# Token groups 4 to 7 normalized in the written order with GpSimd's help, and the token-block steps hung on named units

## The chip, the cores and the metric

The kernel runs on one core of a Trainium2 chip. A core has five engines that work side by side, each through its own queue in order: TensorE (PE in the profile, its weight loads PEld), VectorE (DVE), ScalarE (ACT), GpSimd (POOL) and SyncE (SP), which here only issues DMAs; POOL issues DMAs too. The metric is the device time of one execution in microseconds (us), the median of three executions.

## What is computed

The input `x` has 2048 tokens of 640 channels. It is normalized per token (mean and variance over the 640 channels, no learned scale), and the result `xn` feeds two branches whose sum is added to `x`:

```python
xn = _layernorm(x, axis=-1)
a = einsum("bsd,ed->bse", xn, dft_hid_re);  b = einsum("bsd,ed->bse", xn, dft_hid_im)
y = einsum("ts,bse->bte", dft_seq_re, a) - einsum("ts,bse->bte", dft_seq_im, b)
gate = xn @ W_gate;  up = xn @ W_up                      # 640 -> 1728
out = x + y + ((gate * (gate > 0)) * up) @ W_down        # 1728 -> 640
```

All data are float32. The kernel multiplies in a split form: an operand is divided into a high part (an ACT copy rounded to `float32r`) and a low part (the rest, by a DVE subtraction, `split`, lines 123 to 125), and a product is three matmuls, high by high, high by low, low by high (`mm3`, lines 130 to 132).

## The kernel before, in words

**Three stages.** The first (to about 405 us) multiplies the two 2048x2048 sequence matrices with `xn`; the second is gate and up; the third is the projection by `W_down` and by the hidden matrices. The change is in the first stage alone.

**Tokens.** A group is 256 tokens (two blocks `j` of 128), so there are 8 groups (`NG`), and `NH` = 4 is half of them. `xn` of groups 0 to 3 lies in `xs_early`, of groups 4 to 7 in `xs_late`, high beside low. The output columns are worked through in 4 chunks `c` of 512.

**Units.** The first stage is a list `todo` of units, each with four steps: `load` (DMAs of 512 KB of a sequence matrix into a tile `raw`, or `tk` for a kept one), `prepare` (the high and low part, into one of the 3 buffers `cb` of the pool `ring`, made by `parts`), `run` (the matmuls) and `finish`. `drive(4, 2)` (line 725) goes through the list: at place i it traces `prepare` of unit i-2, `load` of unit i, `finish` of unit i-5 and `run` of unit i-4, so a unit is prepared two units ahead of its matmuls. `defer(k, f)` calls `f` k places later.

The first 16 units are `B11` (groups 0 to 3) and `B21` (groups 4 to 7), for each group once with chunk c=0 and once with c=1 (`first_stream`, line 546). The two units of a group have 18 matmuls each. The tokens of group g+1 are normalized in `prepare` of unit (c=1, group g). After these come the same units for chunks 2 and 3, and then for each chunk c the units `T1`, `T2`, `B22`, `T3`, `T4` (four each, `stream`, line 644; order in lines 771 to 775). `T1` and `B22` units have 18 matmuls, the others 12. `prepare` of a `T` unit has a DVE subtraction (line 672 and following, recorded at line 646) ahead of the split; that of `B22` has the split alone. After the last of four units `combine` (line 614) does 2 to 4 operations of 128x512 on the sums.

**Who sets the order.** The program is traced in the order above; a planner then lays out each engine's queue, moving an instruction forward where it takes its operands to be ready sooner. Two things hold it: `tc.keep_in_program_order` (through `pin`) puts an instruction behind all that was traced on its engine, and `tc.issue_after(ins)` puts a block's instructions on the engine of `ins` behind `ins`. Neither waits for data by itself.

**The two ways to normalize.** Groups 1 to 3 use `next_group` (line 266), pinned: statistics on DVE (`ln_stats`, lines 204 and 205), the unit's high part on ACT (274), the unit's low part in two halves on POOL (272, for g > 1), held back by `behind_vector` (264) until DVE has finished the low part before it, the root (211 to 218), the normalized high part in two ACT operations (281), the centred and scaled tokens in two DVE operations (285), the low part (287). Groups 4 to 7 use `layernorm` (line 237), which isn't pinned but for the queueing behind `late["ln"]`: one block is centred and scaled by DVE (247), the other by ACT (248), then one ACT copy (251, recorded at 121) and one DVE subtraction (252) of both. In `next_group` the high and low part have 384 of the 640 channels per block (`K14`); the other 256 are moved by a DMA (`keep_a21`, 235). In groups 4 to 7 all 640 are made. The matmuls of the c=0 unit of groups 1 to 3 are `next_products` (line 488, recorded at 495), pinned, which start with what is ready first; those of groups 4 to 7 went through `product`.

**Token-block steps.** Six background steps (`token_sets(1, step)`, line 338) make transposed, normalized blocks that the second stage needs. Steps 0 and 1 load `mr` (mean and root rows, broadcast) and `a` by 3 POOL DMAs, do an add and a multiply of 128x512 (364, 365) and a split; steps 2 to 5 load by 4 POOL DMAs (378, 379), do two adds and two multiplies of 128x512 (384, 385), four subtractions of 128x256 (`more`, 391) and two splits of 128x1024, and store the halves by POOL DMAs (422). Their work tiles lie in eight slots (`work`), used in turn. Before the change a step is put into the list 2 units after `V3` and then every `SPACE` = 9 entries: the load at its place, the halves 6 and 7 units later, all arithmetic in one piece.

Of the kernel before, what the change touches and what calls it, by code (L numbers as in the profile page):

```python
# [12 lines left out]
P = 128  # L13
# [45 lines left out]
def fnet_reglu_kernel(  # L59
# [177 lines left out]
    def layernorm(g):  # L237
        xs, bs, mv = ln_tiles(g)
        js = slice(0, SG)

        with tc.issue_after(late["ln"]):
            for i in ln_stats(g, xs, bs, mv, js):
                pass
            for i in ln_root(g, mv, js):
                late["ln"] = i.ins
            nc.vector.tensor_tensor(mv[:, 1, 6:7], stat[:, 0, g, 1:2], stat[:, 1, g, 1:2], op=OP.mult)
            nc.vector.tensor_scalar(xs[:, 0], xs[:, 0], mv[:, 0, 0:1], stat[:, 1, g, 0:1], op0=OP.subtract, op1=OP.mult)
            nc.scalar.activation(xs[:, 1], xs[:, 1], AF.Identity, bias=mv[:, 1, 6:7], scale=stat[:, 1, g, 1:2])
            cs = K14 if g < NH else slice(0, D)
            src = xs[:, :, cs]  # L250
            high = copy(xn_block(g, cs, 0), src)
            low = nc.vector.tensor_tensor(xn_block(g, cs, 1), src, xn_block(g, cs, 0).bitcast(F32), op=OP.subtract)
            if g < NH:
                keep_a21(g)
        if g == NG - 1:
            nc.sync.dma_start(rows.rearrange("m (g p j) -> p m g j", p=P, j=SG), stat)

# [8 lines left out]
    def next_group(g, b, raw, before):  # L266

        xs, bs, mv = ln_tiles(g)
        js = slice(0, SG)
        nm, r = (stat[:, i, g, js] for i in range(2))  # L270
# [10 lines left out]
        pin(nc.scalar.activation(xn_block(g, K14, 0)[:, j], xs[:, j, K14], AF.Identity,  # L281
# [5 lines left out]
        late["ln"] = pin([nc.vector.tensor_tensor(xn_block(g, K14, 1), xs[:, :, K14], xn_block(g, K14, 0).bitcast(F32),  # L287
                                                  op=OP.subtract)])[0].ins
        keep_a21(g)
# [48 lines left out]
    def token_sets(q, step, place=None, unit=None):  # L338
# [30 lines left out]
        else:  # L369
# [11 lines left out]
            def make():  # L381
                mr, ab = t["mr"], t["ab"]
                for i in range(2):
                    tc.keep_in_program_order(tt(part(ab, i), part(ab, i), part(mr, 0), op=OP.add))  # L384
                    tt(part(ab, i), part(ab, i), part(mr, 1), op=OP.mult)
# [23 lines left out]
        def begin():  # L409
            load()  # L410
            for i, (make, name, place, view) in enumerate(made):

                def halve(make=make, name=name):
                    for m in make:
                        m()
                    src = t[name]
                    t["h" + name] = h = work()[:, : src.shape[1]]
                    split(h.bitcast(F32R), src.bitcast(F32R), src)

                def keep(name=name, place=place, view=view):  # L420
                    for v, part in enumerate((t["h" + name], t[name])):
                        nc.gpsimd.dma_start(place(v), view(part))
# [65 lines left out]
    def next_products(n, b):  # L488

        keys = [("e1", 0), ("e1", 1), "v1"]  # L490
        for js, vs in (((0,), (0, 2)), ((1,), (0, 2)), ((0, 1), (1,))):
            for j in js:
                for v in vs:
                    for d, key in zip((0, 1, 4), keys):
                        start["pe"] = pin([nc.tensor.matmul(E[0, key], xn_part(n * SG + j, d)[v == 1], b[:, int(v == 2), j],  # L495
                                                            start=False, stop=n == NH - 1 and (j, v) == (1, 1))])[0].ins
# [49 lines left out]
    def first_stream(c, name, g):  # L546
# [24 lines left out]
        def prepare():  # L571
# [4 lines left out]
            if (n > 0 or c > 1) and "b" not in t:  # L576
                t["b"] = b = parts()
                with ExitStack() as order:
                    if c == 1 and n < NH:
                        order.enter_context(tc.issue_after(late["ln"]))  # L580
                    i = split(flat(b, 0), flat(b, 1), t["s"])
                if c == 1 and n < NH - 1:
                    late["ln"] = i.ins
            if norm is not None:
                if norm < NH:
                    t1 = start[0, norm]
                    t1["b"] = parts()
                    next_group(norm, t1["b"], t1["s"], flat(b, 1)[:, W2 - 1 : W2] if norm > 1 else None)
                else:
                    layernorm(norm)  # L590

        def run():
# [3 lines left out]
            if 0 < n < NH and c == 0:  # L596
# [3 lines left out]
            with ExitStack() as order:  # L600
                if 0 < n < NH and c == 1:
# [42 lines left out]
    def stream(c, name, g):  # L644
# [19 lines left out]
        def prepare():  # L664
# [4 lines left out]
            with in_turn():  # L669
# [13 lines left out]
                lows.append(split(flat(b, 0), flat(b, 1), src))  # L683

# [55 lines left out]
    steps = [(q, i) for q in (1,) for i in range(SET_STEPS)]  # L740
    early_sets, first_sets = list(SETS_A), list(SETS_B)
    free = [None]
    SPACE = 9

    def phase(c, names):


        for n in names.split():
# [12 lines left out]
            if n == "V3":  # L761
                free[0] = len(todo) + 2
            if free[0] is not None and len(todo) >= free[0] and steps:
                token_sets(*steps.pop(0))
                free[0] = len(todo) + SPACE

# [7 lines left out]
    assert not steps, len(steps)  # L774
    phase(NCHUNK - 1, "T10 T11 T12 T13 T20 B220 T21 B221 T22 T23 K K K A A B222 B223 T30 A T31 A T32 A T33 T40 T41 T42 T43 K")
    assert not early_sets and not first_sets
    drive(4, 2)
    ph1.close()
# [522 lines left out]
```

## Time and profile before

| | |
|---|---|
| median of 3 runs | 1040.99 us (1040.63 to 1042.91) |
| the profiled execution, its own time | 1040.59 us |
| its span in the trace | 1038.7 us |
| TensorE busy | 1025.0 us, 99% |
| VectorE busy | 801.3 us, 77% |
| ScalarE busy | 432.1 us, 42% |
| GpSimd busy | 106.9 us, 10% |
| granted TensorE clock | 1.00 |

How to read the profile: times in the trace count from the start of the span. A row of the timeline has the start, the duration, the engine, the line of the kernel, the operation, output and inputs by the program's names, the shapes, the count, and in brackets the idle time of that engine ahead of it with what ended it. A row of the windows has the stretch, its length, and for each engine the busy time and the number of instructions, then the granted clock, the DMA share and GB/s. A row of the operations of one tile has the count, then the shortest, median and longest duration in ns, and the first and last start in us. Matmuls are pipelined: their rows overlap, so lost time is read from the distance of their starts.

### The profile page before, as it was taken

The numbers are of one execution on the slowest core, as the hardware profiler recorded it, in microseconds if no ns is written. First come the engines' busy times: TensorE is split into PE (matmuls) and PEld (weight loads), VectorE is DVE, ScalarE is ACT, GpSimd is POOL, SyncE is SP. The second block draws the span as 40 slices with busy tenths as digits, with TensorE's granted clock in tenths as the row PEclk, the third lists the DMA queues.
The fourth block names the chain that finished last, engine by engine and source line by source line (L and its number), as shares of the span: only waits on it lengthen the run. The fifth ranks groups of instructions, "written<-read, shape, count | busy, mean of one in ns | idle before, by whom it ended". The sixth has DMA issues, their size and how long they took to land.

```text
span 1038.7 us, 12463 instructions
## 1 busy us (share of the span) xinstructions
PE 1025.0 (99%) x4528; PEld 844.2 (81%) x4528; DVE 801.3 (77%) x1074; ACT 432.1 (42%) x544; POOL 106.9 (10%) x172
## 2 busy tenths in 40 slices
PE   9899999999999999999999999999999999999998
PEld 7788888888787888888888888888878888888886
DVE  7857887979979767688887988887498667786764
ACT  6654453333343423333334534433365423552521
POOL 3211000102121001321110010010000000000000
PEclk9999999999999999999999999999999999999999
DMA  8987743947977975763363666663698636986554
GB/s 303 320 284 258 255 141 115 333 171 251 364 239 273 391 304 190 250 237 136 149 233 135 225 223 237 229 248 122 207 367 292 197 120 217 379 299 219 159 157 122
DMA packets 101468, 242.73 MB, mean 234 GB/s; under 512 B 11552, under 2 KB 50976, under 8 KB 98848
## 3 DMA queue, kind: packets, MB, share of 16 engines
q1 hardware_dynamic: 83664, 171.68, 48.2%
q0 software_dynamic: 17744, 70.26, 18.4%
q8 instruction: 35, 0.57, 0.2%
q14 instruction: 25, 0.20, 0.1%
HBM read 182.12 MB, written 58.74 MB: 232 GB/s over the span
## 4 chain that ended last, share of the span: by engine, by line
PE 91%; DVE 5%; DMA 1%; ACT 1%; issue 1%; SPq 0%; DVEq 0%; ACTq 0%
PE ps L132 30%; PE ps L131 30%; PE ps L130 30%; DVE cb L125 1%; PE ps L1198 1%; PE ps L495 1%; DMA rw<-hd 1%; DVE raw L646 1%; DMA raw<-in_dft 1%; DVE r L125 0%; DVE tk L646 0%; ACT cb L124 0%; DVE bs L204 0%; DVE r L391 0%; DVE r L384 0%
## 5 line engine op out<-in xcount | busy, mean ns | idle before, releaser
L130 PE MATMUL ps<-cb,wt 128*128 128x512 f32 x390 | 151.9, 390 | 0.4 <-ACT wt L124 0.4
L132 PE MATMUL ps<-cb,wt 128*128 128x512 f32 x390 | 151.9, 390 | 0.4 <-DVE wt L125 0.4
L131 PE MATMUL ps<-cb,wt 128*128 128x512 f32 x390 | 151.8, 389 | 0.0
L125 DVE TENSOR_TENSOR cb<-rw,cb 128x1024 fp32r<-128x1024 f32 x83 | 94.1, 1134 | 69.3 <-ACT cb L124 68.7
L124 ACT ACTIVATE cb<-rw 128x1024 fp32r<-128x1024 f32 x83 | 81.9, 987 | 149.9 <-PE ps L132 124.8
L124 ACT ACTIVATE cb<-raw 128x1024 fp32r<-128x1024 f32 x75 | 79.4, 1060 | 132.1 <-PE ps L132 101.6
L125 DVE TENSOR_TENSOR cb<-raw,cb 128x1024 fp32r<-128x1024 f32 x75 | 91.5, 1223 | 42.0 <-ACT cb L124 41.8
L130 PE MATMUL ps<-cb,xs_late 128*128 128x512 f32 x256 | 99.3, 390 | 4.3 <-ACT xs_late L121 2.8
L131 PE MATMUL ps<-cb,xs_late 128*128 128x512 f32 x256 | 100.1, 391 | 1.4 <-DVE cb L125 1.2
L131 PE MATMUL ps<-xs_early,gw 128*128 128x512 f32 x260 | 101.2, 389 | 0.0
L130 PE MATMUL ps<-xs_early,gw 128*128 128x512 f32 x260 | 101.2, 389 | 0.0
L132 PE MATMUL ps<-xs_early,gw 128*128 128x512 f32 x260 | 101.1, 389 | 0.0
L132 PE MATMUL ps<-cb,xs_late 128*128 128x512 f32 x256 | 99.3, 389 | 0.0
L121 ACT ACTIVATE gw<-z 128x1024 fp32r<-128x1024 f32 (+1 forms) x52 | 57.6, 1110 | 77.7 <-DVE z L808 75.1
L132 PE MATMUL ps<-cb,xs_early 128*128 128x512 f32 x226 | 87.9, 389 | 0.0
L131 PE MATMUL ps<-cb,xs_early 128*128 128x512 f32 x226 | 87.9, 389 | 0.0
L130 PE MATMUL ps<-cb,xs_early 128*128 128x512 f32 x226 | 87.4, 390 | 0.4 <-ACT cb L124 0.4
L130 PEld LDWEIGHTS ps<-cb,wt 128*128 128x128 f32 x390 | 73.2, 188 | 16.1 <-ACT wt L124 0.9
L132 PEld LDWEIGHTS ps<-cb,wt 128*128 128x128 f32 x390 | 73.2, 188 | 15.9 <-DVE wt L125 0.7
L131 PEld LDWEIGHTS ps<-cb,wt 128*128 128x128 f32 x390 | 73.2, 188 | 15.7 <-DVE cb L125 0.3
L121 ACT ACTIVATE u<-ps 128x512 f32<-128x512 f32 x52 | 31.1, 599 | 93.7 <-PE ps L132 93.7
L818 DVE TENSOR_TENSOR gw<-z,gw 128x1024 fp32r<-128x1024 f32 (+1 forms) x52 | 64.7, 1286 | 3.8 <-ACT gw L121 3.8
(198 smaller groups left out, 1947.7 us busy)
## 6 DMA issues: line engine op xcount, KB each, us to landing
raw<-in_dft SPq DMA_DIRECT2D x94, 512.0 KB, 6.2
wt<-wparts SPq DMA_DIRECT2D x66, 256.0 KB, 3.2
z<-in_wgu SPq DMA_DIRECT2D x26, 640.0 KB, 3.9
hd<-ob POOLq DMA_DIRECT2D x26, 512.0 KB, 3.7
rw<-hd SPq DMA_DIRECT2D x24, 512.0 KB, 6.8
wparts<-pw POOLq DMA_DIRECT2D x11, 1024.0 KB, 4.1
tk<-in_dft SPq DMA_DIRECT2D x16, 512.0 KB, 7.0
set<-r POOLq DMA_DIRECT2D x16, 512.0 KB, 4.6
```

The lines of the kernel that those rows point to most:

```text
L121: return nc.scalar.activation(o, i, AF.Copy)
L124: nc.scalar.activation(hi, src, AF.Copy)
L125: return nc.vector.tensor_tensor(lo, src, hi.bitcast(F32), op=OP.subtract)
L130: nc.tensor.matmul(ps, wh, mh, start=first, stop=False, skip_group_check=more)
L131: nc.tensor.matmul(ps, wh, ml, start=False, stop=False, skip_group_check=more)
L132: nc.tensor.matmul(ps, wl, mh, start=False, stop=last, skip_group_check=more)
L495: start["pe"] = pin([nc.tensor.matmul(E[0, key], xn_part(n * SG + j, d)[v == 1], b[:, int(v == 2), j], start=False, stop=n == NH - 1 and ( ...
L646: sub = lambda o, i0, i1: nc.vector.tensor_tensor(o, i0, i1, op=OP.subtract)
L818: tt(self.w[:, 1, cs], self.z[:, cs], self.w[:, 0, cs].bitcast(F32), op=OP.subtract)
L1198: nc.tensor.matmul(B[key], wr[:, v, es], hr[:, cs], start=False, stop=v == 1, skip_group_check=not new)
```

## The change

Groups 4 to 7 go through `next_group` and `next_products` as well, over all 640 channels; `layernorm` is gone. With that, the `ring` buffer of the c=0 unit is made there too, its low part goes to POOL, and the queueing of the c=1 unit holds for all groups. The token-block steps are no units of their own any more: their loads, makes, `more`, halves and stores are hung on `prepare` of named units. Steps 0 and 1: load at `T1` units 2 and 3 of chunk 0, the rest at `B22` units 0 and 1 of chunk 0. Steps 2 and 3 (c=1), 4 and 5 (c=2): loads at `T3` unit 3 and `T4` unit 1 of the chunk before, one add and multiply at each `T1` unit of chunk c, `more` and the halves at its `B22` units, stores 2 units later.

```diff
@@ first_stream and the groups
-    def layernorm(g):
...
+        cs = K14 if g < NH else slice(0, D)
...
-        pin(nc.scalar.activation(xn_block(g, K14, 0)[:, j], xs[:, j, K14], AF.Identity,
+        pin(nc.scalar.activation(xn_block(g, cs, 0)[:, j], xs[:, j, cs], AF.Identity,
                                  bias=mv[:, j, 6:7], scale=stat[:, 1, g, j : j + 1]) for j in range(SG))
...
-        late["ln"] = pin([nc.vector.tensor_tensor(xn_block(g, K14, 1), xs[:, :, K14], xn_block(g, K14, 0).bitcast(F32),
+        late["ln"] = pin([nc.vector.tensor_tensor(xn_block(g, cs, 1), xs[:, :, cs], xn_block(g, cs, 0).bitcast(F32),
                                                   op=OP.subtract)])[0].ins
-        keep_a21(g)
+        if g < NH:
+            keep_a21(g)
+        if g == NG - 1:
+            nc.sync.dma_start(rows.rearrange("m (g p j) -> p m g j", p=P, j=SG), stat)
...
-                                                            start=False, stop=n == NH - 1 and (j, v) == (1, 1))])[0].ins
+                                                            start=False, stop=n % NH == NH - 1 and (j, v) == (1, 1),
+                                                            skip_group_check=n >= NH)])[0].ins
...
-                    if c == 1 and n < NH:
+                    if c == 1:
                         order.enter_context(tc.issue_after(late["ln"]))
                     i = split(flat(b, 0), flat(b, 1), t["s"])
-                if c == 1 and n < NH - 1:
+                if c == 1 and n < NG - 1:
                     late["ln"] = i.ins
             if norm is not None:
-                if norm < NH:
-                    t1 = start[0, norm]
-                    t1["b"] = parts()
-                    next_group(norm, t1["b"], t1["s"], flat(b, 1)[:, W2 - 1 : W2] if norm > 1 else None)
-                else:
-                    layernorm(norm)
+                t1 = start[0, norm]
+                t1["b"] = parts()
+                next_group(norm, t1["b"], t1["s"], flat(b, 1)[:, W2 - 1 : W2] if norm > 1 else None)
...
-            if 0 < n < NH and c == 0:
+            if n > 0 and c == 0:
                 next_products(n, t["b"])
                 return
...
-                if 0 < n < NH and c == 1:
+                if n > 0 and c == 1:
                     order.enter_context(tc.issue_after(start["pe"]))
@@ token_sets
-            def make():
+            def make(two=range(2)):
                 mr, ab = t["mr"], t["ab"]
-                for i in range(2):
+                for i in two:
                     tc.keep_in_program_order(tt(part(ab, i), part(ab, i), part(mr, 0), op=OP.add))
                     tt(part(ab, i), part(ab, i), part(mr, 1), op=OP.mult)
...
-                defer(6 + i, halve)
-                defer(8 + i, keep)
-
-        todo.append((begin, idle, idle, idle))
+        halves_of = {name: lambda name=name, place=place, view=view: (halve(name), defer(2, lambda: keep(name, place, view)))
+                     for _, name, place, view in made}
+        return load, made[0][0], halves_of
@@ stream, end of prepare
+            for f in hooks.pop((c, name, g), ()):
+                f()
@@ instead of the list of steps and SPACE
+    for step in range(2):
+        load, make, halve = token_sets(1, step)
+        at(0, "T1", 2 + step, load)
+        at(0, "B22", step, *make, halve["a"])
+    for step in range(2, SET_STEPS):
+        load, (make, more), halve = token_sets(1, step)
+        c, i = 1 + (step - 2) // 2, step % 2
+        at(c - 1, *(("T3", 3), ("T4", 1))[i], load)
+        for j in range(2):
+            at(c, "T1", 2 * i + j, lambda make=make, j=j: make((j,)))
+        at(c, "B22", 2 * i, more, *([halve["ab"]] if i else []))
+        at(c, "B22", 2 * i + 1, *([halve["mr"]] if i else halve.values()))
```

More of the change, by code (lines that the diff above doesn't have):

```diff
@@ L407, in token_sets, with halve, keep @@
             return
[L409 to L422, printed above, removed]
-                defer(6 + i, halve)
-                defer(8 + i, keep)
-        todo.append((begin, idle, idle, idle))
+        def halve(name):
+            src = t[name]
+            t["h" + name] = h = work()[:, : src.shape[1]]
+            split(h.bitcast(F32R), src.bitcast(F32R), src)
+        def keep(name, place, view):
+            for v, part in enumerate((t["h" + name], t[name])):
+                nc.gpsimd.dma_start(place(v), view(part))
+        halves_of = {name: lambda name=name, place=place, view=view: (halve(name), defer(2, lambda: keep(name, place, view)))
+                     for _, name, place, view in made}
+        return load, made[0][0], halves_of
     def raw():
@@ L738, in drive, with at @@
         todo.clear()
[L740 removed]
     early_sets, first_sets = list(SETS_A), list(SETS_B)
[L742 to L743 removed]
+    hooks = {}
+    def at(c, name, g, *fs):
+        hooks.setdefault((c, name, g), []).extend(fs)
+    for step in range(2):
[10 more added lines that the diff above has]
+        at(c, "B22", 2 * i + 1, *([halve["mr"]] if i else halve.values()))
     def phase(c, names):
```

25 lines of the change are left out of this document (1 added, 24 removed).

## The prediction

> **What bounds the kernel now.** The page comes first: busy times, then the granted clock.
>
> ```profile
> PE 1025.0 (99%) x4528; PEld 844.2 (81%) x4528; DVE 801.3 (77%) x1074; ACT 432.1 (42%) x544; POOL 106.9 (10%) x172
> ```
>
> TensorE is the bound; the change adds and removes no matmul, so it can win only TensorE's pauses. The second view is TensorE's timeline: first the pace without a pause, then the three places with an idle time that lie in the first stage behind its start-up.
>
> ```profile
> 24.36 4.24 PE L495 MATMUL ps<-cb,xs_early 128*128 128x512 f32 x18
> 28.44 0.39 PE L130 MATMUL ps<-cb,xs_early 128*128 128x512 f32 x1
> ...
> 40.45 0.39 PE L132 MATMUL ps<-cb,xs_early 128*128 128x512 f32 x1
> 43.69 0.50 PE L130 MATMUL ps<-cb,xs_late 128*128 128x512 f32 x1 [2.85 <-ACT xs_late L121]
> 44.03 0.40 PE L131 MATMUL ps<-cb,xs_late 128*128 128x512 f32 x1
> ...
> 269.40 0.39 PE L132 MATMUL ps<-cb,xs_late 128*128 128x512 f32 x1
> 271.20 0.73 PE L130 MATMUL ps<-cb,xs_late 128*128 128x512 f32 x2 [1.41 <-ACT cb L124]
> 272.34 0.97 PE L130 MATMUL ps<-cb,xs_early 128*128 128x512 f32 x3 [0.41 <-ACT cb L124]
> 273.44 0.50 PE L131 MATMUL ps<-cb,xs_late 128*128 128x512 f32 x1
> 273.77 0.39 PE L132 MATMUL ps<-cb,xs_late 128*128 128x512 f32 x1
> ...
> 329.48 0.39 PE L132 MATMUL ps<-cb,xs_late 128*128 128x512 f32 x1
> 329.90 0.73 PE L130 MATMUL ps<-cb,xs_late 128*128 128x512 f32 x2
> 331.85 0.50 PE L131 MATMUL ps<-cb,xs_late 128*128 128x512 f32 x1 [1.22 <-DVE cb L125]
> 332.19 0.40 PE L132 MATMUL ps<-cb,xs_late 128*128 128x512 f32 x1
> ```
>
> Eighteen matmuls start within 28.44 - 24.36 = 4.08 us, 0.227 each; so a unit of 18 takes 4.08 us, one of 12 takes 2.72, a group (two units) 8.16. What a pause costs is the distance of starts less 0.227 per matmul. First place (40.45 to 44.03, 2 steps): 3.58 - 0.45 = 3.13. Second (269.40 to 273.77, 7 steps): 4.37 - 1.59 = 2.78. Third (329.48 to 332.19, 4 steps): 2.71 - 0.91 = 1.80. Together 7.7 us: the most that this change can win. The first is TensorE waiting for the normalized high part of group 4 (what `layernorm` makes), the other two for cut operands at the end of chunks 1 and 2.
>
> The third view asks what VectorE does there: busy time by stretch, then the token-block tile `r` on VectorE in the first of these stretches.
>
> ```profile
> 250.80:272.60 21.80, 19.98 (x87) 15.95 (x86) 21.44 (x27) 9.79 (x10) 4.02 (x6) 1.00 0.91 322
> 316.10:339.70 23.60, 22.35 (x98) 17.66 (x97) 23.60 (x29) 9.10 (x9) 4.68 (x7) 1.00 0.79 300
> 383.20:405.00 21.80, 21.80 (x98) 18.06 (x97) 17.87 (x19) 7.88 (x9) 1.62 (x3) 1.00 0.73 257
> ```
>
> ```profile
> L391 DVE TENSOR_TENSOR r<-r x4: 422/423/425, 260.5 to 262.6; 128x256 f32<-128x256 f32 x4
> L384 DVE TENSOR_TENSOR r<-r x2: 686/686/687, 255.8 to 258.1; 128x512 f32<-128x512 f32 x2
> L385 DVE TENSOR_TENSOR r<-r x2: 687/687/687, 257.5 to 259.9; 128x512 f32<-128x512 f32 x2
> L125 DVE TENSOR_TENSOR r<-r x2: 1226/1227/1228, 264.1 to 265.2; 128x1024 fp32r<-128x1024 f32 x2
> ```
>
> The columns behind the length are PE, PEld, DVE, ACT and POOL. The `T3`/`T4` stretch (eight units of 12) of chunk 3 has no token-block step: VectorE 17.87 of 21.80, TensorE never idle. In chunks 1 and 2 a whole step lies in it: 2 x 0.686 + 2 x 0.687 + 4 x 0.423 + 2 x 1.227 = 6.9 us of rows, some 6.1 of queue time, since successive rows overlap by about 0.08. VectorE is then full and TensorE loses 2.78 and 1.80 us.
>
> **The change, first part: the steps.** It adds no arithmetic and no DMA; 6.1 us per step leave the `T3`/`T4` stretches, where a unit offers 2.72 us and needs a subtraction and a low part, both of 128x1024 like the last row, 2 x 1.227 less the overlap, 2.3. They go beside `T1` and `B22` units of 4.08 us. One add and multiply is 0.686 + 0.687 less the overlap, 1.2 us, so a `T1` unit needs 3.5; a `B22` unit needs 1.14 plus, in the four of a chunk, 1.35, 2.3, 2.5 and 1.14, so 3.6 at most. None is over 4.08. A chunk's `T2`/`B22` stretch gets 4 x 1.14 + 8 x 0.34 = 7.3 us of the two steps, where chunk 1 had 6.1 without a pause, with this load:
>
> ```profile
> 223.60:250.80 27.20, 27.20 (x121) 22.52 (x120) 24.16 (x28) 10.40 (x10) 4.57 (x7) 1.00 0.50 181
> ```
>
> 24.16 + 1.2 = 25.4 of 27.2: I cost it at nothing. What is late next is the first `T1` unit of a chunk, since it is prepared during `T4`, where the sums of `T3` (four operations) also fall due. Chunk 1 shows its margin:
>
> ```profile
> 205.80 2.36 DVE L125 TENSOR_TENSOR cb<-tk,cb 128x1024 fp32r<-128x1024 f32 x2
> ...
> 207.04 0.39 PE L130 MATMUL ps<-cb,xs_early 128*128 128x512 f32 x1
> ```
>
> The first low part is done at 206.94, the matmul that reads it starts at 207.27: 0.33 us, with step 1's add, multiply and split (1.8 us) ahead of it. Step 1 moves to `B22`, so the margin becomes 2.1, and the same at the next two chunk ends. The new add and multiply stands behind that low part, ahead of the second unit's, which is due 4.08 later. So I take both pauses as gone: -4.6 us; if VectorE stays late at one of the two ends, half of it.
>
> The loads are POOL DMAs in the same number, pinned to nothing; a make at the head of VectorE's queue would wait for them. Their nearest rows:
>
> ```profile
> 249.99 0.73 POOL L379 DMA_DIRECT2D r<-in_xt  x1 [3.35 <-DMA set<-r]
> ...
> 252.69 0.72 POOL L378 DMA_DIRECT2D r<-rows  x1 [1.25 <-issue]
> ```
>
> ```profile
> r<-rows POOLq DMA_DIRECT2D x12, 256.0 KB, 6.2
> ```
>
> From a wait for the eight-slot tile's store to the last landing it is 252.69 - 246.6 + 6.2 = 12 us. By the diff a load stands five units ahead of its make, at least 5 x 2.72 = 13.6 us. So I cost it at nothing, with 1 to 2 us of cover; the planner may also bring it forward. The price without cover is rival five.
>
> **Second part: groups 4 to 7.** It removes the pause of 3.13 us if group 4 is ready at 40.68. The pinned chain is read from group 2, on VectorE, then ACT and POOL:
>
> ```profile
> 19.50 0.88 DVE L204 BATCH_NORM_STATS2 bs<-r 128x6 f32<-128x320 f32 x2
> ...
> 23.85 1.21 DVE L285 TENSOR_SCALAR r<-r,mv,stat 128x640 f32<-128x640 f32 x2 [0.78 <-ACT xs_early L281]
> 25.10 0.96 DVE L287 TENSOR_TENSOR xs_early<-r,xs_early 128x768 fp32r<-128x768 f32 x1
> ...
> 27.11 0.88 DVE L204 BATCH_NORM_STATS2 bs<-r 128x6 f32<-128x320 f32 x2
> ```
>
> ```profile
> 23.11 1.31 ACT L281 ACTIVATE xs_early<-r,mv,stat 128x384 fp32r<-128x384 f32 x2
> ...
> 36.94 1.06 ACT L124 ACTIVATE cb<-raw 128x1024 fp32r<-128x1024 f32 x1
> ...
> 38.69 1.07 ACT L121 ACTIVATE sa<-ps 128x512 f32<-128x512 f32 x2
> ...
> 40.60 0.93 ACT L248 ACTIVATE r<-r,mv,stat 128x640 f32<-128x640 f32 x1
> ```
>
> ```profile
> 35.19 1.27 DVE L204 BATCH_NORM_STATS2 bs<-r 128x6 f32<-128x320 f32 x3
> ...
> 43.67 1.49 DVE L252 TENSOR_TENSOR xs_late<-r,xs_late 128x1280 fp32r<-128x1280 f32 x1
> ```
>
> ```profile
> 19.82 2.54 POOL L272 TENSOR_TENSOR cb<-raw,cb 128x512 fp32r<-128x512 f32 x2
> ```
>
> Group 2 takes 27.11 - 19.50 = 7.61 us from statistics to statistics. Groups 4 to 7 differ in width: the low part 1.49 in place of 0.96 (+0.53), and ACT's two high parts 2 x 0.93 in place of 1.31 (+0.55, since the second of 285 waits for the second of them). So 8.7 us per group against TensorE's 8.16. GpSimd takes the low part of the c=0 unit off VectorE: it starts behind VectorE's last low part and lies beside the statistics and the root, 2.54 us.
>
> Group 4's statistics start at 35.19 as now. By group 2 the high part starts 3.61 later, 38.8; ACT's copy of a unit (36.94) and of the sums (38.69) stand near the root and push it by 0.5 to 0.8, an estimate from these two rows. The first block's high part is then ready at 40.4 to 40.6, TensorE needs it at 40.68, the second's 1.36 later. The low part, read from the 13th matmul on (+2.72, 43.4), is done at about 43.2. So the pause goes, with 0.2 us in hand, and the chain then loses 8.7 - 8.16 = 0.54 per group for three groups: 1.6 - 0.2 = 1.4 us of new pauses by group 7. Bounds: nothing (the chain keeps TensorE's pace) and 3.1 (the pause only moves). I take 1.4, since both widths have rows. Net -3.13 + 1.4 = -1.7.
>
> At nothing: `next_products` has the same 18 matmuls, only in another order; the statistics' store on SP comes some 8 us later, in front of loads of units whose matmuls are over 10 us away; on POOL the new low parts wait for VectorE's low part before them, and behind them are queued the stores of the sums and the loads of the steps, which serve nothing that TensorE reads for tens of us.
>
> **Sum.** 1040.59 (the profiled execution, 1038.7 of span and 1.9 around it) - 4.6 - 1.7 = 1034.3. The median of the three runs is 0.4 above the profiled one: 1034.7.
>
> **Rivals.**
> 1. All three pauses vanish: 7.7 less, 1033.3. For it: if ACT's copies fall behind the high parts, the first is ready at 38.8 + 0.93 = 39.7, 1.0 us in hand, and only 0.6 of the 1.6 is left (1033.9). Against it: 8.7 over 8.16, and the copies' place before the change.
> 2. The change does not do what it says at group 4: the planner leaves ACT's copy of the c=1 sums, which end at 40.7, ahead of the high parts. The first high part is ready at 40.7 + 0.2 + 0.55 + 0.93 = 42.4, a pause of 1.7, and the chain's 1.6 comes on top: 3.3 in place of 1.4, the pause is moved, not removed. 1034.7 + 1.9 = 1036.6. The copies at 38.69 already stand ahead of ACT's part of the normalizing (40.60).
> 3. VectorE stays late at one chunk end, since `T1` units now need 3.5 of 4.08 and the sums come too: half of 4.6 stays, 1037.0.
> 4. GpSimd and VectorE hold each other up. In group 2 the low part at 19.82 lies beside statistics with one tensor input and shows nothing; if it comes later by one of its halves, it lies beside the subtractions. If each then waited for half a low part (2.54 / 2 = 1.27), four groups lose 5.1 more: 1039.8, no change. [...] No row here shows such a wait. The order "behind VectorE's low part" speaks against it.
> 5. Slower: a make waits for its loads. Place: VectorE's queue at `T1` units 0 and 2 of chunks 1 and 2, if POOL issues the four loads only behind the stores of the `T4` sums at a chunk's end. Price: 12 us to land, less the 2 to 4 us in hand and the 4 us of the unit, some 4 us for each of four steps, 16 in all: 1051. The gain of 6.3 is spent at a loss of 1.6 per step. Against it: by the diff the loads stand ahead of these stores; for it: only the planner's clock places them.
>
> **How the numbers follow.** Forecast 0.47 (its own range 1033.9 to 1036.2), rivals 0.12, 0.13, 0.08, 0.06 and 0.14. A measurement of this kernel tells 0.2% (2 us) from no change. Forecast and rivals 1 to 3 are faster: 0.80; rival 4 is within: 0.06; rival 5 slower: 0.14. The range reaches from all 7.7 won with 0.6 for the spread of runs, 1032.7, to rival 4, 1039.8.
>
> **What would show it.** Steps: no idle time of TensorE near 270 and 330, and `r` operations in the `T3`/`T4` stretches gone. Groups: no pause at 40.7, small ones of 0.2 to 0.5 near 49, 57 and 65, 8.7 us from statistics to statistics, POOL rows of 2.54 beside them. Wrong would be a VectorE row of 384 that waits for a DMA, a wait of 1.27 beside a POOL row, or ACT's sum copies ahead of line 281.

## The result and the profile after

The changed kernel takes 1033.01 us (median of 4 runs, 1032.58 to 1033.63), the kernel before in the same set 1041.72 (4 runs, 1040.63 to 1042.91): ratio 0.992, 95% interval 0.9906 to 0.9933. The profiled execution is the one of 1033.63 us, with a span of 1031.9; before it was 1040.59 and 1038.7. So the traces account for 6.8 us, and the medians moved by 8.7; the difference is taken up in the last experiments.

The page first, busy times of the changed kernel:

```profile
PE 1024.6 (99%) x4528; PEld 844.7 (82%) x4528; DVE 801.1 (78%) x1074; ACT 430.1 (42%) x544; POOL 117.3 (11%) x184
```

VectorE and ScalarE do what they did before, 801.1 and 430.1 us (801.3 and 432.1 before); GpSimd has some 10 us more, the new low parts. TensorE's work is the same to 0.4 us, so the gain can only be pauses of TensorE. Its timeline, at the last matmul of group 3 and at the first one of each of the four chunks and of the second stage:

```profile
40.25 0.39 PE L132 MATMUL ps<-cb,xs_early 128*128 128x512 f32 x1
...
139.97 0.39 PE L130 MATMUL ps<-cb,xs_early 128*128 128x512 f32 x1
...
205.25 0.39 PE L130 MATMUL ps<-cb,xs_early 128*128 128x512 f32 x1
...
270.53 0.39 PE L130 MATMUL ps<-cb,xs_early 128*128 128x512 f32 x1
...
335.81 0.39 PE L130 MATMUL ps<-cb,xs_early 128*128 128x512 f32 x1
...
401.09 0.39 PE L130 MATMUL ps<-xs_early,wr 128*128 128x512 f32 x1
```

All four distances are 65.28 us, which is 288 matmuls of 0.2267: no chunk loses anything any more. Before, the same five milestones stood at 141.76, 207.04, 272.34, 340.14 and 408.07 (at 272.34 and 340.14 the first matmuls of the new chunk are mixed with the last of the old one; the last number is clean). That gives the account of the 6.8 us:

- From the last matmul of group 3 to the first of chunk 0: 101.31 before (141.76 - 40.45), 99.72 after (139.97 - 40.25): **1.6** from the groups.
- From there to the second stage: 266.31 before (408.07 - 141.76), 261.12 after (401.09 - 139.97): **5.2** from the steps.
- The start up to group 3 is 0.2 earlier (40.25 against 40.45), and the part behind 401 is 0.2 longer: nothing in all.

VectorE's windows of the changed kernel show where the steps went: the `T1` and the `T2`/`B22` stretch of chunk 1, then the `T3`/`T4` stretches of chunks 1 and 2 (stretch, length, then PE, PEld, DVE, ACT, POOL, clock, DMA share, GB/s); below it the same time in the kernel before, whose own `T1` stretch lies 1.8 us later (207.04 to 223.36, with VectorE busy for 11.67).

```profile
205.25:221.57 16.32, 16.32 (x73) 13.52 (x72) 16.30 (x22) 8.38 (x9) 2.07 (x3) 1.00 0.64 230
221.57:248.78 27.21, 27.21 (x122) 22.53 (x121) 23.52 (x26) 9.45 (x9) 6.63 (x9) 1.00 0.70 231
248.78:270.53 21.75, 21.75 (x97) 18.02 (x96) 20.67 (x22) 8.50 (x8) 5.25 (x8) 1.00 0.97 349
314.06:335.81 21.75, 21.75 (x97) 18.02 (x96) 20.67 (x21) 8.50 (x8) 1.63 (x3) 1.00 0.98 348
```

```profile
205.25:221.57 16.32, 16.32 (x73) 13.49 (x72) 12.02 (x12) 5.54 (x6) 0.54 (x1) 1.00 0.72 272
```

Beside `T1` VectorE was busy for 12.02 of 16.32 us and is now for 16.30: full, and TensorE still doesn't stop. Beside `T3`/`T4` it had 27 and 29 instructions and has 22 and 21 now, with 1.1 us to spare, and TensorE is at 21.75 of 21.75. The token-block tile `r` alone, on VectorE, in the three stretches of chunk 1 (stretch, length, busy time), before and then after (with the windows moved by 1.8 us the kernel before has 0.00, 6.45 and 6.46):

```profile
205.25:221.57 16.32, 0.00 (x0) 1.00 0.72 272
221.57:248.78 27.21, 6.45 (x10) 1.00 0.46 166
248.78:270.53 21.75, 6.46 (x10) 1.00 0.91 334
```

```profile
205.25:221.57 16.32, 7.09 (x12) 1.00 0.64 230
221.57:248.78 27.21, 4.63 (x7) 1.00 0.70 231
248.78:270.53 21.75, 1.37 (x2) 1.00 0.97 349
```

5.1 us left the last stretch and 1.8 the one before it; 7.1 went beside `T1`. The 1.37 that stay are the first add and multiply of chunk 2, since a unit is prepared ahead of its matmuls. A stretch may be full as long as its own work is due later than its end; the busy share alone doesn't tell.

The groups, on VectorE: the statistics of groups 4 to 7, and the end of the normalizing of group 4.

```profile
35.00 0.88 DVE L204 BATCH_NORM_STATS2 bs<-r 128x6 f32<-128x320 f32 x2
...
39.65 0.61 DVE L265 TENSOR_SCALAR r<-r,mv,stat 128x640 f32<-128x640 f32 x1 [1.01 <-ACT xs_late L261]
40.46 0.62 DVE L265 TENSOR_SCALAR r<-r,mv,stat 128x640 f32<-128x640 f32 x1 [0.20 <-ACT xs_late L261]
41.11 1.49 DVE L267 TENSOR_TENSOR xs_late<-r,xs_late 128x1280 fp32r<-128x1280 f32 x1
...
43.66 0.88 DVE L204 BATCH_NORM_STATS2 bs<-r 128x6 f32<-128x320 f32 x2
...
46.81 0.17 DVE L214 RECIPROCAL mv<-mv 128x2 f32<-128x2 f32 x1 [1.04 <-ACT mv L211]
...
52.91 0.88 DVE L204 BATCH_NORM_STATS2 bs<-r 128x6 f32<-128x320 f32 x2
...
61.52 0.88 DVE L204 BATCH_NORM_STATS2 bs<-r 128x6 f32<-128x320 f32 x2
```

```profile
38.70 1.72 ACT L261 ACTIVATE xs_late<-r,mv,stat 128x640 fp32r<-128x640 f32 x2
40.33 1.06 ACT L121 ACTIVATE sa<-ps 128x512 f32<-128x512 f32 x2
...
45.54 1.06 ACT L124 ACTIVATE cb<-raw 128x1024 fp32r<-128x1024 f32 x1 [1.74 <-PE ps L471]
```

```profile
35.39 2.54 POOL L252 TENSOR_TENSOR cb<-raw,cb 128x512 fp32r<-128x512 f32 x2
```

ScalarE's high parts (line 261) now stand ahead of its copy of the c=1 sums (line 121); they had stood behind it. From statistics to statistics the groups take 8.66, 9.25 and 8.61 us. The middle one is longer since ScalarE's copy of a unit at 45.54 waited 1.74 us for TensorE to free the buffer, and the root, on ScalarE too, came behind it: the 1.04 us that VectorE waits at 46.81. TensorE's pauses in the groups sum to 139.97 - 40.48 - 432 x 0.2267 = 1.56 us, cut so small that none is among its waits. They are of two kinds. The first unit of group 4, then the next one's start:

```profile
40.48 4.88 PE L471 MATMUL ps<-cb,xs_late 128*128 128x512 f32 x18
...
45.20 0.39 PE L130 MATMUL ps<-cb,xs_late 128*128 128x512 f32 x1
```

That is 4.72 us for 18 matmuls that need 4.08. The 0.6 us are lost at 40.96 and 41.44, right behind the ends of ScalarE's two copies of the sums (the row at 40.33), for which two weight loads of TensorE wait (0.8 us in all): these copies now stand behind the high parts. The other kind is the chain: by the distances of starts 0.4 us each in groups 6 and 7, behind VectorE's and ScalarE's normalizing, and nothing in group 5.

### The profile page after: what moved, and what is told of

The parts are those of the page before. It is cut to its first block, busy times and chain, and to the rows that moved or that the text cites. A ratio compares the mean times of both kernels' runs of the same rounds, so it can differ in the third digit from the quotient of the medians.

```text
span 1031.9 us, 12494 instructions
## 1 busy us (share of the span) xinstructions
PE 1024.6 (99%) x4528; PEld 844.7 (82%) x4528; DVE 801.1 (78%) x1074; ACT 430.1 (42%) x544; POOL 117.3 (11%) x184
## 4 chain that ended last, share of the span: by engine, by line
PE 96%; DVE 2%; DMA 1%; ACT 1%; issue 0%; SPq 0%; DVEq 0%; ACTq 0%
PE ps L132 31%; PE ps L131 31%; PE ps L130 31%; PE ps L471 3%; PE ps L1183 1%; DMA rw<-hd 1%; DVE bs L204 0%; DMA r<-in_x 0%; ACT xs_late L261 0%; ACT xs_early L261 0%; ACT mv L212 0%; DVE mv L205 0%; DVE r L265 0%; DVE cb L125 0%; SPq L1190 0%
## 5 line engine op out<-in xcount | busy, mean ns | idle before, releaser
L124 ACT ACTIVATE cb<-raw 128x1024 fp32r<-128x1024 f32 x71 | 75.3, 1061 | 123.0 <-PE ps L132 106.3
L125 DVE TENSOR_TENSOR cb<-raw,cb 128x1024 fp32r<-128x1024 f32 x71 | 86.7, 1222 | 35.7 <-ACT cb L124 35.5
L130 PE MATMUL ps<-cb,xs_late 128*128 128x512 f32 x232 | 90.2, 389 | 0.0
L131 PE MATMUL ps<-cb,xs_late 128*128 128x512 f32 x232 | 90.2, 389 | 0.0
L132 PE MATMUL ps<-cb,xs_late 128*128 128x512 f32 x232 | 90.2, 389 | 0.0
```

Source lines behind the costliest of these rows:

```text
L124: nc.scalar.activation(hi, src, AF.Copy)
L125: return nc.vector.tensor_tensor(lo, src, hi.bitcast(F32), op=OP.subtract)
L130: nc.tensor.matmul(ps, wh, mh, start=first, stop=False, skip_group_check=more)
L131: nc.tensor.matmul(ps, wh, ml, start=False, stop=False, skip_group_check=more)
L132: nc.tensor.matmul(ps, wl, mh, start=False, stop=last, skip_group_check=more)
```

## The experiments

**Theory**: the two parts act apart. The steps win because VectorE has slack beside `T1` and `B22` and had none beside `T3`/`T4`; the groups win because a written order puts the high parts where TensorE needs them. **Rivals**: the planner's order shifts because the steps' entries leave the list of units, whatever the place; GpSimd's help, not the order, carries the groups; and the cover that the prediction named (hold, early loads) isn't needed.

### One part alone

groups_only takes the diff without its steps, steps_only the steps without the groups.

> The groups' part alone, the steps as before the change. Theory (two separate causes that add up): the pause of 3.13 us at 40.7 goes and 1.5 us of small pauses come between 41 and 70, as in the changed kernel, so about 1.6 us faster than before; the two pauses at the ends of chunks 1 and 2 (together 5.2 us by the distance of TensorE's starts) stay. Rival (the parts help each other: an earlier start gives VectorE a lead that lasts to the chunk ends): over 3 us faster, with shorter pauses at the chunk ends.

> The steps' part alone, groups 4 to 7 as before the change. Theory (adds up): no pause of TensorE at the ends of chunks 1 and 2, the pause of 3.1 us at 40.7 stays; 5.2 us faster than before. Rival (the parts help each other): less than 4 us, with a pause left at a chunk end.

Measured, beside 1041.27 for the kernel before (21 runs): groups alone 1039.2 us, ratio 0.9979 (0.997 to 0.9988); steps alone 1037.17, ratio 0.9958 (0.9944 to 0.9971). TensorE's waits of the two, releaser in the middle, then us in all, times, longest; first groups alone, then steps alone:

```profile
PE ps L130 <- ACT cb L124: 1.8, 2, 1.4
PE ps L131 <- DVE cb L125: 1.5, 1, 1.5
```

```profile
PE ps L130 <- ACT xs_late L121: 2.8, 1, 2.8
```

Each part leaves exactly the other's pauses: 1.4, 0.4 and 1.5 us at the chunk ends in the first, 2.8 at 43.67 in the second. In the traces the second stage starts at 406.35 and at 402.91 in place of 408.07, so 1.7 and 5.2 us; both together 408.07 - 401.09 = 7.0. In the traces the parts add up. The medians don't: 2.1 and 4.1 us, where idle_entries of the same set, which has both parts, has 8.1. The section on the medians takes this up.

### The place of the steps

idle_entries puts six empty entries into the list of units, one for each step of the old list. steps_in_t4 keeps the new hooks, but hangs the second step of each chunk on the first two `T4` units:

```diff
+            if n == "V3":
+                spots_left.extend((len(todo) + 2, SET_STEPS))
+            if spots_left and spots_left[1] and len(todo) >= spots_left[0]:
+                todo.append((idle, idle, idle, idle))
+                spots_left[:] = len(todo) + 9, spots_left[1] - 1
...
+    spots_left = []
```

```diff
-        at(c - 1, *(("T3", 3), ("T4", 1))[i], load)
+        if i:
+            at(c, "T2", 0, load)
+            at(c, "T4", 0, make, more, halve["ab"])
+            at(c, "T4", 1, halve["mr"])
+            continue
+        at(c - 1, "T3", 3, load)
```

> The changed kernel with six empty entries put back into the list of units, at the places where the steps stood before. An empty entry takes a place of the list, so the unit next to it is prepared only one real unit ahead of its matmuls in the traced order. Theory (VectorE's work in the T3/T4 stretches made the pauses, not the entries): same time as the changed kernel, 1033.0 within 0.5, no pause at the chunk ends. Rival (the entries took the lead): pauses of 1 to 3 us at the ends of chunks 1 and 2 come back, 1035 to 1038.

> The changed kernel with all arithmetic of steps 3 and 5 hung on T4 units 0 and 1 of chunks 1 and 2 (as hooks, no entries of the list), loads at T2 unit 0. Theory (the place of the 6.1 us of VectorE's work decides): the pauses of 2 to 3 us at the ends of chunks 1 and 2 come back, 1037 to 1038.5, VectorE full in the T3/T4 stretches. Rival (it is the list's entries or the single piece of arithmetic at a bad moment of the planner, not the stretch): no pause, 1033.0 within 0.5.

Measured: 1033.22 us (ratio 0.9923, 0.9909 to 0.9936) and 1040.41 (0.9995, 0.9987 to 1.0004). The entries do nothing; the place of two steps of six is worth 7.2 us. The windows of steps_in_t4 at the end of chunk 1 and the start of chunk 2:

```profile
250.50:272.30 21.80, 20.72 (x91) 16.51 (x89) 21.08 (x26) 8.50 (x8) 2.08 (x3) 1.00 0.84 297
272.30:288.60 16.30, 14.99 (x65) 12.12 (x66) 16.09 (x20) 7.39 (x8) 4.74 (x7) 1.00 0.79 289
```

VectorE is back at 21.08 of 21.80 with 26 instructions, TensorE stops for 1.08 us by its busy time, and for 1.31 more in the next `T1` stretch: full in the changed kernel too, but with nothing owed from the stretch before it. By distances of starts each of the two chunk ends costs 3.2 us (0.93 + 0.51 + 1.44 at the first, at 269.43, 272.33 and 274.57, and 0.11 in the matmul behind each), so 6.4 of the 7.2. That is more than I had set: I had counted the stretch alone and not the full one behind it.

### What carries the groups

low_on_vector leaves the low part of the c=0 unit of groups 4 to 7 on VectorE, at the place that next_group has for it. no_wait keeps GpSimd and takes away a wait: line 265 writes over the tile that ScalarE's high parts (line 261) still read, so its first instruction waits until ScalarE is done; here it writes into the place of the low part, and the subtraction reads it from there.

```diff
-                next_group(norm, t1["b"], t1["s"], flat(b, 1)[:, W2 - 1 : W2] if norm > 1 else None)
+                next_group(norm, t1["b"], t1["s"], flat(b, 1)[:, W2 - 1 : W2] if 1 < norm < NH else None)
```

```diff
-        pin(nc.vector.tensor_scalar(xs[:, j], xs[:, j], ...
-        late["ln"] = pin([nc.vector.tensor_tensor(xn_block(g, cs, 1), xs[:, :, cs], xn_block(g, cs, 0)...
+        whole = xs if g < NH else xn_block(g, cs, 1).bitcast(F32)
+        pin(nc.vector.tensor_scalar(xn_block(g, cs, 1)[:, j] if g >= NH else xs[:, j], xs[:, j], ...
+        late["ln"] = pin([nc.vector.tensor_tensor(xn_block(g, cs, 1), whole[:, :, cs], xn_block(g, cs, 0)...
```

> The changed kernel, but the low part of the c=0 unit of groups 4 to 7 goes back from GpSimd to VectorE, behind the normalized high parts. Theory (the order counts, not GpSimd): VectorE idles there for 1.2 us per group, waiting for ACT, and the 1.14 us of the low part fit in: same time as the changed kernel within 0.4. Rival (GpSimd's help carries the gain): the chain grows by 1.1 us per group, 3 to 4 us of pauses more, 1036 to 1037.

> The changed kernel, but in groups 4 to 7 VectorE writes the centred and scaled tokens into the place of the low part instead of over its input, so that it needn't wait until ACT has read that input. Theory (the pauses of 1.5 us between 40 and 70 come from a chain of 8.6 us per group against TensorE's 8.16): the chain falls by the 0.6 us that the second operation and its wait stand in it, to 8.0, the pauses shrink to under 0.5 us, 1.0 us faster than the changed kernel, 1032.0. Rival (the pauses come from ACT's queue, where a copy that waits for TensorE stands ahead of the root): same time as the changed kernel, within 0.3.

> The changed kernel once more, to stand beside the three that follow on the same chip. Both theories: 1033.0 within 0.6, small pauses of TensorE between 40 and 70 of 1.5 us in all.

Measured in one set, beside 1041.39 for the kernel before (15 runs): the changed kernel again 1034.03 us (1032.15 to 1036.96, ratio 0.9929, 0.9913 to 0.9946), low_on_vector 1033.08 (0.9923, 0.9905 to 0.994), no_wait 1031.6 (1031.52 to 1032.64; 0.9906, 0.9891 to 0.9922). The changed kernel lies 1.0 above its first set here, more than the 0.6 expected, with a span that is only 0.1 longer in its profile (1032.0). VectorE in low_on_vector, group 6:

```profile
56.38 0.16 DVE L260 TENSOR_TENSOR mv<-stat 128x2 f32<-128x2 f32 x1
56.49 1.23 DVE L252 TENSOR_TENSOR cb<-raw,cb 128x1024 fp32r<-128x1024 f32 x1
57.63 1.33 DVE L265 TENSOR_SCALAR r<-r,mv,stat 128x640 f32<-128x640 f32 x2
59.00 1.49 DVE L267 TENSOR_TENSOR xs_late<-r,xs_late 128x1280 fp32r<-128x1280 f32 x1
```

The low part of 1.23 us fills the very time in which VectorE waits for ScalarE in the changed kernel (the 1.01 and 0.20 at 39.65 and 40.46 above); the second stage starts at 401.09, as in the first profile of the changed kernel. GpSimd's help is worth nothing here (the median is even 0.95 lower, with runs that overlap): the written order carries the 1.6 us. Which half of it, the normalizing of `next_group` or the matmuls' order of `next_products`, no run separates. That VectorE has time to wait there speaks for doing away with the wait. The same engine in no_wait, one group, shows what comes of it:

```profile
43.15 0.88 DVE L204 BATCH_NORM_STATS2 bs<-r 128x6 f32<-128x320 f32 x2
...
46.70 1.13 DVE L266 TENSOR_SCALAR xs_late<-r,mv,stat 128x640 fp32r<-128x640 f32 x2
48.59 1.49 DVE L268 TENSOR_TENSOR xs_late<-xs_late 128x1280 fp32r<-128x1280 f32 x1 [0.76 <-ACT xs_late L261]
...
51.14 0.88 DVE L204 BATCH_NORM_STATS2 bs<-r 128x6 f32<-128x320 f32 x2
```

The subtraction of the mean no longer waits, the chain takes 7.99 us per group, under TensorE's 8.16, and the second stage starts at 400.30, 1.0 earlier than in the changed kernel of this set (401.32). TensorE's pauses in the groups shrink from 1.4 to 0.6 us by the distances of starts; what is left is the wait for ScalarE's copies of the sums. The median is 2.4 us lower; the rest is in the third stage, where the pauses near 748 to 750 are 1.3 us shorter in this trace. The edit doesn't explain that, and two profiles of the unchanged kernel before (the second is before_third, below) differ by 0.9 in the same place. By its median it is the fastest of the versions tried, though its runs overlap with those of the changed kernel.

### The cover that the prediction counted on

no_hold lets GpSimd start before VectorE's last low part is done (`if g < NH:` ahead of the hold of line 243); late_loads hangs a step's loads on the first of its own `T1` units, in the written order of POOL, in place of five units earlier:

```diff
         if before is not None:
-            behind_vector(before)
+            if g < NH:
+                behind_vector(before)
```

```diff
+                    move = (lambda *a: pin([nc.gpsimd.dma_start(*a)])) if q else nc.gpsimd.dma_start
...
-        at(c - 1, *(("T3", 3), ("T4", 1))[i], load)
+        at(c, "T1", 2 * i, load)
```

> The changed kernel without the hold that keeps GpSimd's low part of groups 4 to 7 behind VectorE's low part before it; GpSimd then starts as soon as ACT's high part is done, beside VectorE's subtractions with two inputs. Rival four of the prediction (the two engines hold each other up for one instruction): VectorE rows of 1.22 and 1.49 beside a GpSimd row become up to 1.3 us longer or start that much later, 2 to 5 us of pauses more. Theory (no lock that is seen): rows of unchanged length within 0.1, same time as the changed kernel within 0.4.

> The changed kernel with the four loads of each of the steps 2 to 5 hung on the same T1 unit as the first add, and kept in the traced order of POOL's queue, so that they can't be brought forward. Rival five of the prediction (an add at the head of VectorE's queue waits for its loads): rows of VectorE that wait for a DMA, pauses of TensorE of 3 to 5 us per step, 1045 to 1051. Theory (the planner knows the loads' time and puts the adds further back among VectorE's other work): adds later by 5 to 10 us, pauses under 2 us in all, 1033 to 1035.

**The hold.** no_hold takes 1038.15 us (1037.5 to 1041.33; ratio 0.9974, 0.9962 to 0.9985), some 4 to 5 us over the changed kernel; chunk 0 starts at 145.04, 4.8 later than in the changed kernel of the same set (140.20). VectorE, then GpSimd, near groups 4 and 6:

```profile
34.12 3.90 DVE L125 TENSOR_TENSOR cb<-raw,cb 128x1024 fp32r<-128x1024 f32 x1
...
53.30 1.50 DVE L268 TENSOR_TENSOR xs_late<-r,xs_late 128x1280 fp32r<-128x1280 f32 x1
54.70 2.31 DVE L125 TENSOR_TENSOR cb<-raw,cb 128x1024 fp32r<-128x1024 f32 x1
```

```profile
34.39 2.54 POOL L252 TENSOR_TENSOR cb<-raw,cb 128x512 fp32r<-128x512 f32 x2
...
53.65 4.51 POOL L252 TENSOR_TENSOR cb<-raw,cb 128x512 fp32r<-128x512 f32 x2 [4.05 <-ACT cb L254]
```

Line 125 on VectorE takes 1.22 us alone and 3.90 here: it ends at 38.02, 1.09 behind the end of GpSimd's two halves at 36.93, and its 3.90 is near the 1.22 + 2.54 = 3.76 of the two one after the other. At 53.65 the rows of both are longer, 2.31 for 1.22 on the one and 4.51 for 2.54 on the other. No row shows this as idle time: it lies inside the rows' durations. So the rows of no_hold show that the two hold each other up; which of them goes first they don't settle, since VectorE's row at 34.12 starts 0.27 us ahead of GpSimd's and yet ends behind it. My expectation that the hold was not needed fell. Rival 4 of the prediction, 5.1 us for four groups, had the price right to 0.3, in part by luck: it gave each group 1.27, and VectorE's rows of line 125 grow by 2.7, 0, 1.1 and 1.1; what keeps it away is the hold, which puts GpSimd beside the statistics: at 35.00 in the changed kernel, with one input, they take 0.88, as at 52.96 in low_on_vector, where GpSimd has no low part.

**The loads.** late_loads takes 1042.15 us (1040.96 to 1043.23), ratio 1.0 (0.999 to 1.0009) to 1042.2 for the kernel before (13 runs): the whole gain is spent. VectorE's waits in the first stage, then its timeline at the first of the four:

```profile
DVE r L368 <- DMA r<-in_xt: 13.2, 4, 4.9
```

```profile
208.59 0.69 DVE L368 TENSOR_TENSOR r<-r 128x512 f32<-128x512 f32 x1 [4.93 <-DMA r<-in_xt]
```

Four waits, 13.2 us, up to 4.93 each: rival 5's mechanism. TensorE loses less than VectorE waits: chunk 1 starts at 205.40, chunk 2 at 276.12 where 270.68 would be its pace (5.44 lost), chunk 3 at 344.70 where 341.40 would be (3.30 lost): 8.7 in all, 2.2 per step. By the price shown next, 1.6 of it is a fall of the clock (0.50 from 217.60 to 221.00). The rival's price, 16 us, was twice too high, and my own expectation, that the planner would put the makes back for under 2 us, fell.

### Why the medians moved by more than the traces

The last runs profile the kernel before twice more, and steps alone once more.

> The kernel before once more, for a second profile. Theory: the same three pauses at 40.7, 271 and 332 within 0.3 us each; what differs from run to run lies elsewhere (the first DMAs, the start of the third stage near 755). Rival: the pauses at the chunk ends themselves differ by over 1 us between runs.

> The steps' part alone once more, for a second profile; its runs spread from 1034.6 to 1037.6. Theory (the pause of 2.85 us at 40.7 lets TensorE's granted clock fall to 0.50 for 3.4 us in some executions, as in the second profile of the kernel before, which costs 1.7 us): either no fall and 1034.6 within 0.5, or a fall right behind the pause at 43.7 and 1036.3 or more. Rival (the spread has nothing to do with the clock): a time of 1036 to 1037.6 with the clock at 1.00 throughout.

> The kernel before, third profile. Theory: as for the steps alone, 1040.6 within 0.5 without a fall of the clock and 1042.3 or more with one behind the pause at 43.7. Rival: a time of 1042 or more with the clock at 1.00 throughout.

The kernel before took 1042.61 us in before_again, with a span of 1040.7, and 1039.85 (1038.0) in before_third, 0.25 under what I had set for it; steps alone took 1036.54 (1034.8), where their first profile had 1034.62. TensorE's three pauses are the same in all three profiles of the kernel before (2.85 or 2.86 at group 4, 1.4 and 1.2 at the chunk ends). TensorE's timeline of before_again behind the pause at group 4, then the window of the same time (the eighth figure is the granted clock):

```profile
40.54 0.39 PE L132 MATMUL ps<-cb,xs_early 128*128 128x512 f32 x1
43.78 0.80 PE L130 MATMUL ps<-cb,xs_late 128*128 128x512 f32 x1 [2.86 <-ACT xs_late L121]
44.37 0.63 PE L131 MATMUL ps<-cb,xs_late 128*128 128x512 f32 x1
...
46.93 0.53 PE L132 MATMUL ps<-cb,xs_late 128*128 128x512 f32 x1
47.30 0.39 PE L130 MATMUL ps<-cb,xs_late 128*128 128x512 f32 x1
```

```profile
43.80:47.20 3.40, 3.40 (x8) 2.72 (x9) 3.23 (x10) 1.59 (x5) 0.55 (x1) 0.50 0.96 339
```

For 3.4 us the granted clock is 0.50, and 8 matmuls run where 15 would. It costs 1.6 to 1.7 us: chunk 0 starts 99.67 us behind the matmul at 43.78, and 98.07 behind the one at 43.69 in the first profile of the same kernel. steps_only_again shows a fall in the same place, with a granted clock of 0.55 from 43.70 to 47.20 and 0.77 from 43.70 to 51.20. Over all the profiles of this study the clock fell in three of the six of kernels with a pause of 2.4 us or more, and in none of the eight whose longest pause is 1.6 or less; the changed kernel is among the eight. So the pause at group 4 costs its 3.1 us and, some of the time, 1.6 to 1.7 more.

What sets the three with a fall apart from the other three was not shown. The length of the pause is not it alone: 2.86 in before_again and 2.4 in late_loads have a fall behind them, 2.85 in the first profile of the kernel before and 2.8 in steps_only have none. No run varies the pause on purpose, so this is what 14 profiles show and no more.

How often the clock falls can be told from the runs, since each in the later sets has its mean clock on record: in the profiled ones 0.998 goes with a fall, 0.999 and 1.000 with none. By this sign 34 of 49 runs of the kernel before had a fall (0.998 or less; median 1042.15 us, the other 15 have 1040.01), and 1 of the 10 of the changed kernel. But groups alone, without the pause at group 4, still shows it in 6 of its 11 runs (1040.13 against 1038.16 for the other five), and steps alone, with it, in 4 of 5. So each part alone leaves falls, and only both together take nearly all of them away, which goes with medians of the parts that add up to less than both. The sign is a mean over the whole run: where the falls of groups alone lie no profile shows. With falls in 34 of 49 and in 1 of 10 runs the difference would be 6.8 + 0.6 x 1.7 = 7.8 us, an estimate; the medians moved by 8.7, 8.1 (idle_entries) and 7.4 (changed_again) in their sets.

## Why the prediction was right, and where it was not

- **TensorE's pauses are all there is to win**: right. 6.8 us in the traces of the 7.7 that were counted. What a pause can cost beyond its own length, the fall of the clock behind it (1.6 to 1.7 us where there was one), was not among the terms.
- **Steps, 4.6 us**: the mechanism was right, the size came out 5.2. The term was read from two places, 2.78 and 1.80; the other 0.6 us lay in places that weren't counted: 0.33 at 341, where TensorE waits once more for a low part of VectorE's behind the end of chunk 2, 0.1 at 327.7, and the rest in distances too long by 0.03 or less.
- **No new pause at `T1`**: right, with VectorE at 16.30 of 16.32 us. The margin at the first `T1` unit of a chunk was put at 2.1 us; the low part before chunk 2 is done at 267.67 and read at 270.76, so it is 3.1:

```profile
266.44 1.23 DVE L125 TENSOR_TENSOR cb<-tk,cb 128x1024 fp32r<-128x1024 f32 x1
267.58 0.69 DVE L367 TENSOR_TENSOR r<-r 128x512 f32<-128x512 f32 x1
```

- **The `T2`/`B22` stretch**: 25.4 of 27.2 us for VectorE predicted, 23.52 measured. Too high, on the safe side: part of what was counted there lies beside `T1`, in which 7.09 us of `r` stand where four adds and four multiplies, 5.5, were expected.
- **Groups, 1.7 us**: 1.6 measured. The pause at 40.7 is gone, as predicted. The new pauses, 1.56 us where 1.4 were expected, agree partly by luck. The first high part is ready at about 39.6, 0.9 ahead of TensorE and not 0.2, because ScalarE's copies fell behind the high parts, as rival 1 had it; the chain of 8.7 us (8.66, 9.25 and 8.61) then costs 0.8 in groups 6 and 7. The copies put back cost 0.6 at group 4, by a wait that no term and no rival had.
- **GpSimd's low part** was counted as relief for VectorE, and that is the reason that failed: without it the time is the same. The relief lies in a time in which VectorE waits anyway.
- **Rivals**: 1 was half right: its condition came about, and its price of what is left of the chain, 0.6, is near the 0.8 measured, but the pauses don't all vanish. 2 did not come about, since ScalarE's high parts (38.70) got ahead of its sums (40.33), nor did 3: no chunk end keeps a pause. 4 and 5 are both real, shown by the longer rows of no_hold (3.90 for 1.22) and the waits of late_loads (up to 4.93); the hold and the five units of lead were the reasons that they stayed away, and the prediction named both. 5 was priced at 16 us where 8.7 would be lost.
- **The total**: 1034.3 by the sum, 1033.63 for the profiled execution: 0.6 from the steps. The step from there to the median, 0.4 upwards, came out 0.6 downwards. In the kernel before the profiled run had no fall of the clock and most others do; in the changed kernel none of the four had one, and that the profiled run is the slowest of them is chance. So 1033.01 lies below the forecast's own range, 1033.9 to 1036.2, next to the 1033.3 of rival 1, without all pauses being gone. Nothing in the single trace of before could show this, as the clock did not fall there.

## What to carry to other kernels

Where one engine is the bound, list its pauses and ask in which stretch the late engine is overfull; work that serves nothing soon is then hung on stretches whose own work is due late, and the stretch behind it counts too. An instruction that waits only since it overwrites what another still reads is moved for the price of another place to write: that was worth more here (1.0 us in the traces) than a second engine (nothing). Where two engines hold each other up, as VectorE and GpSimd did in no_hold, it need not show as idle time (1.22 us became 3.90 inside the row): compare a row's duration with that of the same shape alone.

## What the runs showed of the hardware that was not expected

The clock's fall: behind pauses of 2.86 us (before_again) and 2.4 (late_loads) the granted clock was 0.50 for 3.4 us (43.80 to 47.20, 217.60 to 221.00), and in steps_only_again 0.55 from 43.70 to 47.20. Pauses of 2.85 (the kernel before, first profile) and 2.8 (steps_only) had none behind them, and what decides no run shows.

VectorE and GpSimd side by side, in no_hold: 1.22 us became 3.90, and 2.54 became 4.51, inside the rows, while statistics with one input beside the same GpSimd instruction kept their 0.88 in the changed kernel. That it is the number of inputs that decides was not shown by itself.
